# Batch 1 of an attention and feed-forward kernel: the number of h matmuls behind each of nine bursts, from a time budget to a written list

## The chip, the core and the metric

The kernel runs on one core of a Trainium2 chip. The metric is the device time of one execution in microseconds (us); the kernel before has a median of 365.38 us over three runs (364.64, 365.38, 365.54). The engines are named as in the profile: PE is the matrix engine (PEld its loading of weights), DVE the vector engine, ACT the scalar engine, POOL the GpSimd engine, SP the queue that issues stores and DMA transposes.

## The reference, cut to what matters

```python
# q, k, v: 8 batches x 12 heads x 448 rows x 64
scores = scale * q @ k.T - log(448)
attn = 1 / (1 + exp(-scores))              # a sigmoid, no softmax
attn_out = attn @ v
x = attn_out as (3584, 768)                # heads side by side
h = x @ w_in                               # w_in: 768 x 2048
g = h * (1 / (1 + exp(-h)))                # SiLU
out = g @ w_out                            # w_out: 2048 x 768
```

## The kernel before, in words

Everything is computed transposed and in 16-bit floats, with 32-bit sums in PSUM. A *group* g is four heads of one batch: three groups to a batch, 24 in all. Of a group there are seven *units* of 64 keys. A unit's `scores` (L253) are four matmuls of 64x448 into one double PSUM bank `psc`, followed by one ACT sigmoid (L267) that writes the tile `attnT`. When all seven units of a group are there, `values` (L275) multiplies them with v in 28 matmuls into two single banks `pav`; two DVE instructions (L302) then bring these into `xT`, the input of the feed-forward part.

The h matmuls of batch b come in 16 *chunks* of 128 hidden columns. `h_unit(b, fc)` (L319) is a generator: it takes one bank `ph`, issues six matmuls of 128x448 with one `yield` after each, and ahead of the last `yield` records what empties the bank. For batch 0 that is an ACT sigmoid (L337) and a DVE product (L338); for batch 1 one ACT SiLU (L342). `first_h` (L588) runs through the 16 chunks of batch 0, then the 16 of batch 1, and between chunks also records pieces of other DVE work (sums of weights, L361 and L512, and copies for later transposes, L216). A chunk of batch 1 can't finish without `xT` of groups 3, 4 and 5; `pairs` (L317) takes group 5's columns last, in the fifth and sixth matmul.

Every engine takes its instructions in the order in which the Python code records them (L53 turns the scheduler off). So the order of the calls is the order of the work. The part that the change touches is L765 to L799. At that point units 0 to 23 have their scores, and chunks 0 and 1 of batch 0 have four of six matmuls each (`begin`, L732). Then come nine *bursts*, n = 24, 26, ..., 40, each the scores of units n and n + 1. `burst` (L777) also issues `values` of a group one burst after the group's last unit: `values(3)` in burst 28, `values(4)` in burst 36; `values(5)` follows the loop at L797. Behind bursts 26 and 30 PE also transposes k and q of group 5 (14 small matmuls and two DVE copies each). Behind each burst `stretch` (L767) runs the stream of h matmuls: each is taken for 189 ns, and it goes on until the sum reaches 1600 ns per burst (900 ns ahead of the first). After `values(5)` the rest of the stream runs without a break (L798), and then the next stage begins: `sets(0)` (L607), whose first instruction on PE is the first product of `out_set` (L536, L539), with bursts of scores between its products.

PSUM has eight banks. In this stage `banks_for_attention(2)` gives two double buffers to `psc` (banks 0 to 3) and four single ones (banks 4 to 7) to all else: `ph`, `pav` and the transposes' `ptr`. A new single tile gets, of the four, the buffer whose last reader was recorded longest ago, and its first matmul waits for that reader. In the next stage `banks_for_attention(3)` (L806) leaves two single buffers, banks 6 and 7; the first product takes bank 6 and the second takes bank 7, and each waits for whoever read that bank last in the stage before.

Of the kernel before, what the change touches and what calls it, by code (L numbers as in the profile page):

```python
# [17 lines left out]
def kernel(  # L18
# [19 lines left out]
    NT_B = NQ * NCH  # L38
# [549 lines left out]
    def first_h():  # L588
        for b in range(2):
            for fc in range(NFC):  # L590
                yield from early[fc] if b == 0 and fc < 2 else h_unit(b, fc)
                if b == 0 and fc >= 10 or b == 1 and fc < 6:
                    next(in_sums)
                if b == 0:
                    continue
                if fc >= 2:
                    next(sums)
                if fc in by_h1:
                    for name in ("k", "q"):
                        dma_transpose(by_h1[fc], name, nc.vector.tensor_copy)  # L600
                    if by_h1[fc] == 8:

                        nc.gpsimd.tensor_copy(gate, qkT["q", 8][:1, 0, :1])
                        for to in (9, 10, 11):
                            load("kq", to)

    def sets(m):  # L607
        for g in range(0, NCH - 1, 2):
            step = out_set(
                block(m, g), row_blocks(m, g), block(m, g + 1), row_blocks(m, g + 1)  # L610
            )
            for i, ns in enumerate(step):
                if m == 0 and g == 0 and i in (10, 14):
                    next(sums)
                if m == 0 and g == 0 and i in (20, 28, 36, 44):
                    next(in_sums)
                yield ns
        if m % 2 == 1:
            g = NCH - 1
            yield from out_set(  # L620
                kept, row_blocks(m - 1, g), block(m, g), row_blocks(m, g), m == B // 2 - 1
            )
# [82 lines left out]
    def values_if_any():  # L705
        if waiting:
            g = waiting.pop(0)
            values(g)
            after_values(g)
            return True  # L710
        return False
# [10 lines left out]
    def transposes(g, name):  # L722
        pe_transpose(g, ((name, 0, 4), (name, 4, NCH)))
        if name == "q":
            after_transpose(g)
# [36 lines left out]
        for do, *what in behind.get(n, ()):  # L762
            do(*what)

    done = due = 0.0  # L765

    def stretch(stream, ns, spent=0):  # L767
        nonlocal done, due
        due += ns
        done += spent  # L770
        while done < due:
            step_ns = next(stream, None)
            if step_ns is None:
                return
            done += step_ns

    def burst(n, size=2):  # L777

        new = units[n : n + size]
        for u in new:  # L780
            scores(*u)
        with_values = values_if_any()
        for g, ch in new:
            if ch == NCH - 1:
                waiting.append(g)
                if 9 <= g + 3 < NQB:
                    later.extend(((g + 3, "k"), (g + 3, "q")))
        return with_values

    stream = first_h()  # L790
    stretch(stream, 900)
    for n in range(NT_B + 3, 2 * NT_B, 2):
        burst(n)
        if n in (26, 30):
            transposes(5, "k" if n == 26 else "q")
        stretch(stream, 1600)
    values_if_any()  # L797
    for _ in stream:  # L798
        pass  # L799
# [5 lines left out]
    for m in range(B // 2 - 1):  # L805
        banks_for_attention(3)  # L806
        nc.scalar.activation(warm, bias_s, AF.Sigmoid)
        stream = sets(m)
# [5 lines left out]
        n = 2 * NT_B * (m + 1)  # L814
# [59 lines left out]
```

## Time and profile before

| what | us |
|---|---|
| three runs: lowest, median, highest | 364.64, 365.38, 365.54 |
| the profiled execution, its time | 364.96 |
| its span (first to last instruction) | 363.2 |
| PE busy in the span | 355.8 (98%) |
| DVE, ACT busy | 252.8 (70%), 249.5 (69%) |
| the nine bursts: first scores of burst 24 to the first matmul of `values(5)` | 28.97 to 53.01 |
| h matmuls without a break behind `values(5)` | 54.46 to 73.96 |
| start of the next stage's first product | 73.96 |
| TensorE clock granted, all slices | 1.00 |

A row of the time-ordered view reads: start, duration, engine, line, operation, written tile <- read tiles, shapes, how many are merged; in brackets the idle time ahead of it and what ended it. A merged row's duration runs from the first start to the last end, so that rows of pipelined matmuls overlap: the next row starts before the one above it ends. The distance of two starts is therefore the better measure on PE.

### The profile page before, as it was taken

What the parts mean: (1) busy time and instruction counts of PE and PEld (TensorE: products, weight loads), DVE (VectorE), ACT (ScalarE), POOL (GpSimd) and SP (SyncE); (2) the same over time, 40 slices, a digit from 0 to 9 for tenths busy, and PEclk for the clock granted to TensorE, in tenths of its full rate; (3) what the DMA queues carried; (4) which work ended last, traced back from release to release, by engine and by line L of the source; (5) the groups of instructions that cost most, each with busy time, mean ns of one, the idle gap of its engine ahead of it and who ended that gap; (6) DMA issues with size and microseconds to landing.
All of it is one profiled execution on the core that took longest, in us unless ns stands there. A gap on an engine that the chain in (4) does not pass through costs nothing. (4 is left out here: it accounts for less than half of the span.)

```text
span 363.2 us, 7671 instructions
## 1 busy us (share of the span) xinstructions
PE 355.8 (98%) x3044; PEld 186.5 (51%) x3044; DVE 252.8 (70%) x461; ACT 249.5 (69%) x341; POOL 76.7 (21%) x115
## 2 busy tenths in 40 slices
PE   7999999999999999999999999999999999999995
PEld 5554445555555555555555455554555555556662
DVE  3665469867666587868566768795856677797763
ACT  6999886489989756688777756679899956640000
POOL 8666421040060272000032047000100000000000
PEclk9999999999999999999999999999999999999999
DMA  9999999989979599008879469602983120003333
GB/s 164 201 202 204 204 204 204 172 116 159 175 109 215 118 133 172 1 2 163 105 133 204 92 138 164 115 2 53 163 102 88 25 65 0 3 0 83 92 88 87
DMA packets 65859, 42.87 MB, mean 118 GB/s; under 512 B 35872, under 2 KB 62496, under 8 KB 65824
## 3 DMA queue, kind: packets, MB, share of 16 engines
q0 software_dynamic: 26800, 22.52, 42.0%
q1 hardware_dynamic: 38320, 19.34, 26.9%
q10 hardware_dynamic: 704, 0.52, 0.4%
q8 instruction: 24, 0.39, 0.4%
q14 instruction: 11, 0.09, 0.1%
HBM read 45.61 MB, written 11.01 MB: 156 GB/s over the span
## 5 line engine op out<-in xcount | busy, mean ns | idle before, releaser
L267 ACT ACTIVATE attnT<-psc,bias_s 128x896 f16<-128x896 f32 x166 | 156.0, 1008 | 20.1 <-PE psc L260 18.8
L539 PEld LDWEIGHTS <-S 128*128 128x128 f16 x448 | 42.0, 98 | 33.6 <-issue 8.1
L260 PE MATMUL psc<-qT,kT 64*64 64x448 f16 x664 | 48.3, 360 | 1.3 <-ACT attnT L245 0.7
L302 DVE TENSOR_SCALAR xT<-pav 128x448 f16<-128x448 f32 x48 | 27.7, 619 | 29.1 <-PE pav L291 29.1
L124 POOL DMA_DIRECT2D vf<-in_v_dram x24 | 17.3, 722 | 131.4 <-PE pav L291 110.0
L539 PEld LDWEIGHTS <-gTr 128*128 128x128 f16 x336 | 31.0, 98 | 27.3 <-issue 8.7
L539 PE MATMUL po<-w_out_sb,gTr 128*128 128x384 f16 x224 | 41.6, 327 | 0.0
L413 PEld LDWEIGHTS <-w_in_sb 128*128 128x128 f16 x288 | 27.9, 98 | 26.7 <-issue 1.1
L539 PE MATMUL po<-T,S 128*128 128x384 f16 x224 | 41.0, 327 | 0.0
L539 PE MATMUL po<-w_out_sb,S 128*128 128x384 f16 x224 | 40.8, 326 | 0.0
L323 PE MATMUL ph<-xT,w_in_sb 128*128 128x448 f16 x192 | 38.5, 353 | 0.0
L291 PE MATMUL pav<-attnT,vf 64*64 64x448 f16 x672 | 38.1, 351 | 0.1
L413 PE MATMUL pa<-xT,w_in_sb 128*128 128x448 f16 x144 | 33.1, 353 | 0.0
L260 PEld LDWEIGHTS <-kT 64*64 64x64 f16 x664 | 17.8, 104 | 27.9 <-issue 21.4
L413 PEld LDWEIGHTS <-SI 128*128 128x128 f16 x216 | 21.1, 98 | 20.0 <-issue 0.5
L291 PEld LDWEIGHTS <-vf 64*64 64x64 f16 x672 | 21.6, 106 | 12.3 <-issue 2.9
L323 PEld LDWEIGHTS <-w_in_sb 128*128 128x128 f16 x192 | 17.8, 98 | 18.9 <-issue 3.4
L429 ACT ACTIVATE part<-pa 128x448 f32<-128x448 f32 x24 | 12.8, 541 | 18.0 <-PE pa L413 18.0
L539 PE MATMUL po<-T,gTr 128*128 128x384 f16 x112 | 21.9, 327 | 0.6 <-DVE osb L560 0.6
L407 ACT ACTIVATE gTr<-pc 128x448 f16<-128x448 f32 x24 | 13.0, 543 | 12.9 <-DVE pc L423 12.5
L423 DVE TENSOR_TENSOR part<-pb,part 128x448 f32<-128x448 f32 x24 | 14.9, 621 | 8.3 <-ACT part L429 5.0
L191 ACT ACTIVATE m<-po 128x384 f32<-128x384 f32 x1 | 0.5, 490 | 27.3 <-PE po L539 27.3
(80 smaller groups left out, 473.2 us busy)
## 6 DMA issues: line engine op xcount, KB each, us to landing
out_dram<-osb SPq DMA_DIRECT2D x52, 192.0 KB, 3.2
vf<-in_v_dram POOLq DMA_DIRECT2D x24, 224.0 KB, 6.5
kf<-in_k_dram POOLq DMA_DIRECT2D x23, 224.0 KB, 6.4
qf<-in_q_dram POOLq DMA_DIRECT2D x23, 224.0 KB, 7.6
w_in_sb<-in_moe_w_in_dram POOLq DMA_DIRECT2D x16, 192.0 KB, 7.9
w_out_sb<-in_moe_w_out_dram POOLq DMA_DIRECT2D x4, 768.0 KB, 14.9
out_dram<-osb SPq DMA_DIRECT2D x6, 96.0 KB, 2.2
kT<-kr SPq DMA_TRANSPOSE x18, 4.8
```

What stands on the lines that cost most here:

```text
L124: nc.gpsimd.dma_start(flat[name, g][:, :, c0:c1].rearrange("p i c d -> p i (c d)"), rows_in(name, g)[:, :, c0 * D : c1 * D],)
L191: nc.scalar.activation(o, i, AF.Copy)
L260: nc.tensor.matmul(psc[own, j, :S], qkT["k", g][rows, ch, own], qkT["q", g][rows, :, own], start=True, stop=True,)
L267: nc.scalar.activation(attnT[g, ch], psc[:, :, :S], AF.Sigmoid, bias=bias_s, scale=QKSCALE)
L291: nc.tensor.matmul(pav[half][j * D : (j + 1) * D, :S], flat["v", g][own, j, ch, :], at[own, j, :], start=(ch == 0), stop=(ch == NCH - 1),)
L302: nc.vector.tensor_scalar_mul(xT[b][:, half * NQ + iq, :], pav[half][:, :S], SX)
L323: nc.tensor.matmul(ph[:, :S], w_in_sb[:, cc, fc * P : (fc + 1) * P], xT[b][:, cc, :], start=(at == 0), stop=(at == NCC - 1),)
L407: nc.scalar.activation(gTr[:, r * NG + i, col + c * S : col + (c + 1) * S], h, AF.Silu, bias=0.0, scale=ISX)
L413: nc.tensor.matmul(to, w[:, n, i * P : (i + 1) * P], x[:, n], start=(start and n == 0), skip_group_check=not start, stop=(n == NQ - 1),)
L423: nc.vector.tensor_add(o, po, x)
L429: nc.scalar.activation(got[i, 1], bank[i, "a"], AF.Copy)
L539: nc.tensor.matmul(po[:, :NO2], a[:, fc, :], w[:, fc, :], start=(fc == 0), stop=(fc == NHC - 1))
```

## The change

The time budget is taken out, and the counts of h matmuls are written into the loop:

```diff
-    done = due = 0.0
-
-    def stretch(stream, ns, spent=0):
-        nonlocal done, due
-        due += ns
-        done += spent
-        while done < due:
-            step_ns = next(stream, None)
-            if step_ns is None:
-                return
-            done += step_ns
-
     stream = first_h()
-    stretch(stream, 900)
-    for n in range(NT_B + 3, 2 * NT_B, 2):
+    for _ in range(5):
+        next(stream)
+    for n, count in zip(range(NT_B + 3, 2 * NT_B, 2), (9, 8, 8, 8, 10, 10, 9, 8, 9)):
         burst(n)
         if n in (26, 30):
             transposes(5, "k" if n == 26 else "q")
-        stretch(stream, 1600)
+        for _ in range(count):
+            next(stream)
     values_if_any()
     for _ in stream:
         pass
```

Nothing else differs. The counts that the budget gave follow from its arithmetic (189 ns a step against 900 + 1600 per burst):

| burst n | ahead | 24 | 26 | 28 | 30 | 32 | 34 | 36 | 38 | 40 |
|---|---|---|---|---|---|---|---|---|---|---|
| what PE does in it besides scores | | | transposes k | values(3) | transposes q | | | values(4) | | |
| h matmuls behind it, before | 5 | 9 | 8 | 9 | 8 | 9 | 8 | 9 | 8 | 8 |
| running sum, before | 5 | 14 | 22 | 31 | 39 | 48 | 56 | 65 | 73 | 81 |
| h matmuls behind it, after | 5 | 9 | 8 | 8 | 8 | 10 | 10 | 9 | 8 | 9 |
| running sum, after | 5 | 14 | 22 | 30 | 38 | 48 | 58 | 67 | 75 | 84 |

The whole stream has 184 steps (192 matmuls less the eight of `begin`); what is not issued in the loop is issued behind `values(5)`. In this count chunk fc of batch 0, from 2 to 15, ends at step 6 fc - 2: chunk 10 at 58, chunk 12 at 70, chunk 13 at 76, chunk 14 at 82, chunk 15 at 88.

## The prediction

> **What bounds the kernel now.** I read the engines' busy times first, then PE's own waits, then the bursts of batch 1 in order of time on PE, ACT and DVE, and last the seam to the next stage.
>
> ```profile
> PE 355.8 (98%) x3044; PEld 186.5 (51%) x3044; DVE 252.8 (70%) x461; ACT 249.5 (69%) x341; POOL 76.7 (21%) x115
> ```
>
> PE is busy 98% of the span, so only what makes PE wait, or spares it a wait, moves the time. These are all its waits for other engines:
>
> ```profile
> PE pw L188 <- DVE bias_s L661: 1.1, 1, 1.1
> PE psc L260 <- ACT attnT L245: 0.7, 1, 0.7
> PE po L539 <- DVE osb L560: 0.6, 1, 0.6
> PE psc L260 <- DVE qT L208: 0.3, 1, 0.3
> PE psc L260 <- ACT attnT L267: 0.2, 1, 0.2
> ```
>
> Only the last lies in the changed stretch. It is in burst 36 (PE in order of time; a gap between rows is left out):
>
> ```profile
> 43.00 1.69 PE L323 MATMUL ph<-xT,w_in_sb 128*128 128x448 f16 x8
> 44.62 0.38 PE L260 MATMUL psc<-qT,kT 64*64 64x448 f16 x4
> 45.24 0.38 PE L260 MATMUL psc<-qT,kT 64*64 64x448 f16 x4 [0.24 <-ACT attnT L267]
> 45.43 1.52 PE L291 MATMUL pav<-attnT,vf 64*64 64x448 f16 x28
> ...
> 50.81 0.65 PE L260 MATMUL psc<-qT,kT 64*64 64x448 f16 x8
> 51.39 1.69 PE L323 MATMUL ph<-xT,w_in_sb 128*128 128x448 f16 x8
> 53.01 1.52 PE L291 MATMUL pav<-attnT,vf 64*64 64x448 f16 x28
> 54.46 7.74 PE L323 MATMUL ph<-xT,w_in_sb 128*128 128x448 f16 x40
> ```
>
> The second unit's scores should start some 0.21 us behind the first's (28 matmuls of values, seven times four, take 54.46 - 53.01 = 1.45, so four take 0.207). They start 0.62 later: PE loses 0.41, of which 0.24 shows as idle. The 40 h matmuls behind values(5) give the price of one: (7.74 - 0.35) / 39 = 0.189 us, without a stall. ACT, and then DVE, over the same stretch:
>
> ```profile
> 42.42 0.98 ACT L337 ACTIVATE tx<-ph 128x448 f16<-128x448 f32 x2
> 43.26 1.93 ACT L267 ACTIVATE attnT<-psc,bias_s 128x896 f16<-128x896 f32 x2
> ...
> 49.12 1.90 ACT L267 ACTIVATE attnT<-psc,bias_s 128x896 f16<-128x896 f32 x2
> 50.92 0.54 ACT L337 ACTIVATE tx<-ph 128x448 f16<-128x448 f32 x1
> 51.34 1.92 ACT L267 ACTIVATE attnT<-psc,bias_s 128x896 f16<-128x896 f32 x2
> 53.12 0.57 ACT L337 ACTIVATE tx<-ph 128x448 f16<-128x448 f32 x1
> ```
> ```profile
> 51.49 0.62 DVE L338 SCALAR_TENSOR_TENSOR gTr<-ph,tx 128x448 f16<-128x448 f32 x1 [1.22 <-ACT tx L337]
> ...
> 53.72 0.62 DVE L338 SCALAR_TENSOR_TENSOR gTr<-ph,tx 128x448 f16<-128x448 f32 x1 [1.14 <-ACT tx L337]
> ```
>
> Burst 36 waits for burst 34's second sigmoid, which ends at 43.26 + 1.93 = 45.19; PE goes on at 45.24, a hop of 0.05. The two L338 rows empty the banks of chunks 12 (until 52.11) and 13 (until 54.34). Chunk 13 is late because its L337 sigmoid stands on ACT behind both sigmoids of burst 40. The seam:
>
> ```profile
> 73.96 2.44 PE L539 MATMUL po<-w_out_sb,gTr 128*128 128x384 f16 x14
> ```
> ```profile
> 74.16 0.54 ACT L342 ACTIVATE gTr<-ph 128x448 f16<-128x448 f32 x1 [0.59 <-PE ph L323]
> ```
>
> The next stage's first product starts 0.74 us before ACT has emptied the bank of batch 1's last chunk (74.70). That works because this chunk lies in bank 7, and the first product takes bank 6.
>
> **The change, part by part.** No instruction is added or removed: 192 h matmuls, 18 units and their evictions stay. Three h matmuls move from behind values(5) to ahead of it, one from behind burst 28 to later, and so three kinds of terms arise. Taking the Python budget out costs nothing on the chip. No DMA moves past another on SP or POOL; their order is the same, and no PE wait above is for a DMA.
>
> *1. Burst 36's stall goes: -0.41.* With one h matmul fewer behind burst 28, burst 32 starts at 40.19 - 0.19 = 40.00; with ten instead of nine behind it, burst 34 at 42.50 as now. ACT, whose chain is psc-bound at burst 32, is 0.19 earlier: burst 34's sigmoids end at 45.00 instead of 45.19. Ten instead of eight h matmuls put burst 36 at 42.50 + 2.12 + 0.38 = 45.00 and its second unit at 45.21, past 45.05. So values(4) starts at 45.40 instead of 45.43, with 58 h matmuls done instead of 56: 0.03 + 2 x 0.189 = 0.41 gained. Chunk 10 now ends ahead of burst 36, so that its L337 (0.54) stands before that burst's sigmoids on ACT, which end near 47.8; burst 38 needs them at about 48.7, so this is hidden by values(4) and nine h matmuls, and would cost at most 0.54 without them. Bounds of the term: 0 and -0.41.
>
> *2. values(5) runs into chunk 13's bank: +1.15.* Burst 40 starts at 50.81 - 0.03 = 50.78, its ACT work likewise 0.03 earlier; nine h matmuls behind it bring values(5) to 53.01 - 0.03 + 0.19 = 53.17. Ahead of it stand 84 steps instead of 81, so chunk 14 is finished and chunk 15 has already taken its bank. Before, values(5)'s two banks are those of chunks 11 and 12, free at 52.11 at the latest. Now chunk 15 has chunk 11's, and values(5) gets those of chunks 12 and 13. Chunk 13's matmuls come earlier only as PE goes: its sixth stands behind burst 40 both times, and its sigmoid behind burst 40's on ACT. So its L338 ends at 54.34 - 0.03 = 54.31, and the first matmul into the second `pav` bank can start at 54.36. The first pair into the other bank goes at 53.17, and then PE stands: 54.36 - 53.17 = 1.19 at most, 1.09 if half a step of four (0.10) was already done. I take 1.15, nearer to the upper, since the last half step runs alone at the end. Queued behind the wait are 26 of 28 values matmuls, chunk 15 and all of batch 1; nothing else feeds PE. What comes next is in time: chunk 0 of batch 1 needs chunk 14's bank (DVE done near 55.3) at 56.5, and xT of group 5 (56.9) at 57.3 and 57.5. Bounds: 0 and 1.19.
>
> *3. The first product of the next stage runs into the last chunk's bank: +0.79.* Four banks go round over the 16 chunks of batch 1, and the round now starts one step on: chunk 0 takes chunk 14's bank, 7, then 4 and 5 (values) and 6 (chunk 15). The last of 16 therefore lies in bank 6, where before it was bank 7. The program as built says the same: its first product now waits for the SiLU of batch 1's last chunk, before for that of three chunks earlier. By the rows above that SiLU ends 74.70 - 73.96 = 0.74 behind the product's start; with the hop of 0.05 PE stands 0.79. The second product (bank 7), eight steps of 0.163 later, no longer waits for it. Bounds: 0 and 0.79.
>
> Sum: -0.41 + 1.15 + 0.79 = +1.53. On the profiled execution's own 364.96 that gives 366.49 (a span of 363.2 + 1.53 = 364.7); this execution lies 0.42 under the median of 365.38, so the median to expect is 366.91. Nothing behind the seam can take it back: PE's waits after 74 us come to 0.6 in all, and a later PE makes ACT and DVE later with it.
>
> **Rivals.**
> *One of the two new waits is hidden.* For it: each rests on one order of banks, and term 2 on an ACT chain. With term 2 alone +0.74 (366.1), with term 3 alone +0.38 (365.8). Against it: term 3 has a margin of 0.79 and term 2 of over 1.0.
> *The bursts get their cover and no bank is late: not slower.* The place is values(5)'s second bank and the first product's; the mechanism is that both evictions end before PE comes. It decides from the point where chunk 13's L338 ends before 53.2, 1.1 earlier than by the rows, and the last SiLU 0.79 earlier or in another bank. Then only term 1 is left: 365.38 - 0.41 = 364.97. The 0.24 of visible idle speaks for it; ACT's order speaks against it.
> *Burst 36 stalls anyway.* Its second unit clears burst 34's sigmoid by only 45.21 - 45.05 = 0.16. Without term 1: +1.94, 367.3.
> *PE runs slower after standing.* The opening 30 filler matmuls of 128 columns (L188) take 3.38 us, where 30 x 128/448 x 0.189 = 1.62 would do: a slow start costs 1.76. If a stall of some 1 us brought that back once: 1.53 + 1.76 = +3.29, 368.7. Against it: after the 0.68 us that PE stands until 7.79, the next filler pairs of 512 columns take 0.60 and 0.60, as later ones do (0.61, 0.60), and the granted clock reads 1.00 in every slice.
> The Trainium skill, page "TensorE: Matmul & The Clock Gate", section "A second HAM failure mode: psum-queue depth-cycling", says that short idle times between groups of matmuls, from waits on PSUM banks, can make the clock gate swing, which would be this rival; the trace's one such gap does not bear it out.
>
> **How the numbers follow.** From no change a measurement of this kernel tells about 0.3%, or 1.1 us: slower means above 366.48. Forecast 0.66, one wait hidden 0.17, no wait 0.07, burst 36 stalls 0.06, slower PE 0.04. The forecast's own range is 366.4 to 367.4 (terms 2 and 3 short by 0.1 or so, medians that spread by 0.4); of its 0.66, 0.06 falls under 366.48. Slower: 0.60 + 0.06 + 0.04 = 0.70. Within: 0.06 + 0.17 + 0.05 = 0.28. Faster by over 1.1: 0.02, out of the no-wait case, since the stretch holds no more than the 0.41 and some 0.1 to gain. The range 365.8 to 367.5 takes in the forecast, the hidden wait and the stalled burst, and leaves out some 0.17.
>
> **What would show it.** Term 1: burst 36 near 45.0 in one row of eight, without idle. Term 2: values(5) broken after two matmuls near 53.2, then idle put down to DVE L338 and going on near 54.36. Term 3: the first L539 row near 75.5, 0.79 later than the h matmuls allow, its idle put down to ACT L342 (less than 0.79 shows, as pipelined ends cover 0.2). Wrong would be: values(5) in one piece, the first product 0.19 behind the last h matmul, or a span under 364.

## The result, and the profile after

| | before | after |
|---|---|---|
| median of 5 runs, us | 365.35 (364.64 to 365.54) | 366.85 (366.66 to 367.40) |
| ratio of the times, 95% interval | | 1.0045 (1.0033 to 1.0056) |
| the profiled execution, its time and span | 364.96, 363.2 | 367.40, 365.4 |
| burst 24's first scores to the next stage's first product | 28.97 to 73.96: 44.99 | 29.59 to 76.14: 46.55 |

The change makes the kernel 1.50 us slower. The last row is the fairest measure of it: inside one execution, the stretch that the change touches takes 46.55 - 44.99 = 1.56 us longer. Behind it the two traces run alike (the next bursts start 2.37 behind the first product before, 2.36 after). The other 0.6 us between the two spans lies ahead of burst 24 (29.59 against 28.97), in code that is the same; the last section comes back to it. Below, *the stretch* always means this distance.

PE's waits after: burst 36's is gone from the list, and two stand there that it didn't have.

```profile
PE pw L188 <- DVE bias_s L661: 1.1, 1, 1.1
PE pav L291 <- DVE gTr L338: 0.8, 1, 0.8
PE psc L260 <- ACT attnT L245: 0.7, 1, 0.7
PE po L539 <- ACT gTr L342: 0.6, 1, 0.6
```

PE in order of time, from burst 34 to values(4), then burst 40 and values(5), then the seam:

```profile
43.12 0.57 PE L260 MATMUL psc<-qT,kT 64*64 64x448 f16 x8
43.62 2.07 PE L323 MATMUL ph<-xT,w_in_sb 128*128 128x448 f16 x10
45.62 0.57 PE L260 MATMUL psc<-qT,kT 64*64 64x448 f16 x8
46.02 1.49 PE L291 MATMUL pav<-attnT,vf 64*64 64x448 f16 x28
...
51.38 0.65 PE L260 MATMUL psc<-qT,kT 64*64 64x448 f16 x8
51.96 1.88 PE L323 MATMUL ph<-xT,w_in_sb 128*128 128x448 f16 x9
53.77 0.38 PE L291 MATMUL pav<-attnT,vf 64*64 64x448 f16 x2
54.97 1.51 PE L291 MATMUL pav<-attnT,vf 64*64 64x448 f16 x26 [0.82 <-DVE gTr L338]
```
```profile
73.83 1.68 PE L323 MATMUL ph<-xT,w_in_sb 128*128 128x448 f16 x8
76.14 1.14 PE L539 MATMUL po<-w_out_sb,gTr 128*128 128x384 f16 x6 [0.63 <-ACT gTr L342]
```

Burst 36 is one row of eight without idle. values(5) breaks after two matmuls: the pair for the first bank goes at 53.77, the second bank's at 54.97, 1.20 later. At the seam the eight h matmuls from 73.83 would let the next instruction start at 73.83 + 8 x 0.189 = 75.34; the product starts at 76.14, 0.80 later. The bracketed idle is smaller both times (0.82 and 0.63), because the ends of pipelined matmuls cover the rest.

What ended the two waits, on DVE and on ACT:

```profile
54.30 0.62 DVE L338 SCALAR_TENSOR_TENSOR gTr<-ph,tx 128x448 f16<-128x448 f32 x1 [1.14 <-ACT tx L337]
```
```profile
51.91 1.92 ACT L267 ACTIVATE attnT<-psc,bias_s 128x896 f16<-128x896 f32 x2
53.69 1.01 ACT L337 ACTIVATE tx<-ph 128x448 f16<-128x448 f32 x2
...
75.54 0.54 ACT L342 ACTIVATE gTr<-ph 128x448 f16<-128x448 f32 x1 [0.59 <-PE ph L323]
```

The L338 row empties chunk 13's bank and ends at 54.92; PE goes on at 54.97. Its L337 sigmoid is the first of the two at 53.69, right behind burst 40's sigmoids. The last SiLU ends at 76.08; the product follows at 76.14.

### The profile page after: what moved, and what is told of

Same layout as the page of the kernel before. It is cut to its first block, busy times and chain, and to the rows that moved or that the text cites. A ratio compares the mean times of both kernels' runs of the same rounds, so it can differ in the third digit from the quotient of the medians.

```text
span 365.4 us, 7671 instructions
## 1 busy us (share of the span) xinstructions
PE 356.8 (98%) x3044; PEld 187.0 (51%) x3044; DVE 252.9 (69%) x461; ACT 249.5 (68%) x341; POOL 76.7 (21%) x115
## 5 line engine op out<-in xcount | busy, mean ns | idle before, releaser
L260 PE MATMUL psc<-qT,kT 64*64 64x448 f16 x664 | 48.1, 360 | 1.0 <-ACT attnT L245 0.7
L260 PEld LDWEIGHTS <-kT 64*64 64x64 f16 x664 | 17.7, 104 | 27.4 <-issue 20.9
L423 DVE TENSOR_TENSOR part<-pc,part 128x448 f32<-128x448 f32 x24 | 15.0, 624 | 6.1 <-PE pc L413 5.5
```

What stands on the lines that cost most here:

```text
L260: nc.tensor.matmul(psc[own, j, :S], qkT["k", g][rows, ch, own], qkT["q", g][rows, :, own], start=True, stop=True,)
L423: nc.vector.tensor_add(o, po, x)
```

## The experiments

Each run was timed beside the kernel before on the same chip (its medians there: 365.32 for runs 1 to 4, 365.03 for runs 5 to 7, 365.12 for runs 8 to 10). The stretch is the finer measure: a median differs from what its stretch says by up to 0.44 us, runs 3, 4 and 6 aside (run 5 lies 0.81 over the kernel before, its stretch 0.37), and the openings alone differ by up to 0.97 (last section). The counts named are those behind the nine bursts; the changed kernel has 9, 8, 8, 8, 10, 10, 9, 8, 9.

| run | stretch expected, us | stretch measured | median, us | ratio to before, 95% |
|---|---|---|---|---|
| before | | 44.99 | 365.35 | |
| after | | 46.55 | 366.85 | 1.0045 (1.0033 to 1.0056) |
| 1: after, 81 steps | 44.70 | 44.67 | 365.00 | 0.9993 (0.9984 to 1.0002) |
| 2: before, 84 steps | 46.54 | 46.59 | 366.89 | 1.0041 (1.0028 to 1.0055) |
| 3: after, other bank at the seam, first filler | 45.81 | 45.80 | 376.87 | 1.0317 (1.0303 to 1.0331) |
| 4: before, other bank at the seam, first filler | 45.83 | 45.83 | 376.01 | 1.0290 (1.0276 to 1.0304) |
| 5: after, chunk 13 early | 45.34 | 45.36 | 365.84 | 1.0015 (1.0005 to 1.0024) |
| 6: as 5 and 3 together, first filler | 44.60 | 44.61 | 375.31 | 1.0285 (1.0271 to 1.0298) |
| 7: chunk 13 early, 81 steps | 44.50 | 44.53 | 364.82 | 0.9991 (0.9983 to 1.0000) |
| 8: as 3, second filler | 45.81 | 45.80 | 365.74 | 1.0013 (0.9998 to 1.0027) |
| 9: as 4, second filler | 45.83 | 45.83 | 366.15 | 1.0023 (1.0009 to 1.0037) |
| 10: as 6, second filler | 44.60 | 44.61 | 364.88 | 0.9987 (0.9973 to 1.0001) |

**Run 1: take back only the three steps.**

```diff
-    for n, count in zip(range(NT_B + 3, 2 * NT_B, 2), (9, 8, 8, 8, 10, 10, 9, 8, 9)):
+    for n, count in zip(range(NT_B + 3, 2 * NT_B, 2), (9, 8, 8, 8, 10, 10, 9, 8, 6)):
```

> The changed counts up to burst 38, but 6 instead of 9 behind burst 40, so that 81 steps stand ahead of values(5) as before. I measure the stretch from burst 24's first scores to the next stage's first product, which the opening doesn't touch: 44.99 us before, 46.55 after. Theory (three separate terms): chunk 15 has not begun, so values(5) gets the banks of chunks 11 and 12 and the last chunk of batch 1 lies away from bank 6; both new waits are gone and term 1 alone is left, less about 0.12 because chunk 15 now comes 0.12 ahead of chunk 13's bank: 44.99 - 0.41 + 0.12 = 44.70, the time 0.3 under before (365.1). Rival (ten matmuls behind two bursts cost time by themselves, or gain nothing): 44.99 or more.

Both waits are gone. The stretch is 44.67, so the longer cover of bursts 32 and 34 is worth 0.32 by itself:

```profile
53.25 1.52 PE L291 MATMUL pav<-attnT,vf 64*64 64x448 f16 x28
54.70 19.77 PE L323 MATMUL ph<-xT,w_in_sb 128*128 128x448 f16 x103
74.31 2.44 PE L539 MATMUL po<-w_out_sb,gTr 128*128 128x384 f16 x14
```

values(5) is in one piece. The 103 h matmuls take 74.31 - 54.70 = 19.61 where before they took 73.96 - 54.46 = 19.50: the 0.11 is what chunk 15 loses on chunk 13's bank. So what costs time in the changed kernel is not that the bursts' counts are uneven, but what comes with 84 steps instead of 81 ahead of values(5): other banks. (Run 10 has 84 steps too and loses nothing in the stretch.)

**Run 2: put only the three steps into the kernel before** (its counts are 9, 8, 9, 8, 9, 8, 9, 8, 8; here 11 come last).

```diff
-    for n, count in zip(range(NT_B + 3, 2 * NT_B, 2), (9, 8, 8, 8, 10, 10, 9, 8, 9)):
+    for n, count in zip(range(NT_B + 3, 2 * NT_B, 2), (9, 8, 9, 8, 9, 8, 9, 8, 11)):
```

> The counts of before, but 11 instead of 8 behind burst 40, so that 84 steps stand ahead of values(5) while burst 36 still stalls. Theory (values(5)'s second bank is free at a time that ACT and DVE set, whenever PE comes): PE comes at 53.58 instead of 53.17, the bank is free at 54.39, PE waits 0.76 instead of 1.15, the product waits 0.79: 44.99 + 1.55 = 46.54, as in the changed kernel; the 0.41 of term 1 is then not worth anything in it. Rival (the prediction's own arithmetic for a stalled burst 36, where the terms add up): 44.99 + 1.94 = 46.93.

```profile
45.24 0.38 PE L260 MATMUL psc<-qT,kT 64*64 64x448 f16 x4 [0.24 <-ACT attnT L267]
...
53.58 0.38 PE L291 MATMUL pav<-attnT,vf 64*64 64x448 f16 x2
54.40 1.51 PE L291 MATMUL pav<-attnT,vf 64*64 64x448 f16 x26 [0.45 <-DVE gTr L338]
```

Burst 36 stalls as before, PE comes to values(5) 0.43 later (24.61 behind burst 24, in the changed kernel 24.18), and goes on at 54.40. In the changed kernel that point lies 54.97 - 29.59 = 25.38 behind burst 24, here 54.40 - 28.97 = 25.43. Both times it lies 3.59 behind burst 40's first scores (51.38 there, 50.81 here), and these start at nearly the same time, 21.79 and 21.84 behind burst 24. From there on ACT's three sigmoids and DVE's product set it, and not whether 9 or 11 h matmuls stand behind the burst. So nearly all of what the change gains in burst 36 is spent waiting 1.20 instead of 0.82 two bursts later: beside run 2's counts it is worth 46.59 - 46.55 = 0.04.

**Runs 3, 4 and 6: another bank for batch 1's last chunk.** A filler matmul ahead of that chunk takes the bank that would have been the chunk's (run 3 with the changed counts, run 4 with those of before, run 6 with those of run 5):

```diff
             for fc in range(NFC):
+                if b == 1 and fc == NFC - 1:
+                    keep_busy(1, P)
                 yield from early[fc] if b == 0 and fc < 2 else h_unit(b, fc)
```

> The changed kernel with one filler matmul of 128 columns (0.05) into a single bank of its own ahead of batch 1's last chunk, which so moves from bank 6 to bank 7. Theory (the first product waits for its bank): the 0.79 at the seam goes, the wait of values(5) stays: 46.55 - 0.79 + 0.05 = 45.81, time about 366.1. Rival (the product is late for another reason, such as the last SiLU's data or ACT's load of a table): 46.60.

> The kernel before with the same filler matmul at the same place, which moves batch 1's last chunk from bank 7 to bank 6. Theory: the seam's wait comes alone: 44.99 + 0.79 + 0.05 = 45.83, time about 366.2, with PE's idle ahead of the first product put down to ACT L342. Rival (the wait comes from the new counts, not from the bank): 45.04.

> The run before this with the filler matmul ahead of batch 1's last chunk: 84 steps ahead of values(5), and neither wait by theory: 45.34 - 0.79 + 0.05 = 44.60, time about 365.0. Rival (three more h matmuls ahead of values(5) cost time by themselves): above 45.2.

The stretches came out as expected, yet the kernels were 10 us slower: a miss in the making of the experiment. `keep_busy` multiplies `dummy`, and `dummy` lies in the buffer that the weight sum `T3` takes later (tag "T3", L182 and L503). With a reader so late, DVE stood before its first write there, and all its sums and copies for the next stage with it (DVE and PE in run 3):

```profile
73.99 0.56 DVE L512 TENSOR_TENSOR T<-w_out_sb 128x768 f16<-128x768 f16 x1 [14.01 <-PE pw L188]
```
```profile
80.50 0.96 PE L260 MATMUL psc<-qT,kT 64*64 64x448 f16 x8 [3.14 <-DMA qT<-qr]
81.40 0.82 PE L539 MATMUL po<-w_out_sb,gTr 128*128 128x384 f16 x2
87.05 2.08 PE L539 MATMUL po<-T,S 128*128 128x384 f16 x6 [4.83 <-DVE m L550]
```

The times of these three runs say nothing about the seam.

**Runs 8, 9 and 10: the same with operands that nobody overwrites soon.**

```diff
+                if b == 1 and fc == NFC - 1:
+                    pw = one_bank("pw")
+                    nc.tensor.matmul(pw[:, :P], w_in_sb[:, 0, :P], xT[1][:, 0, :P], start=True, stop=True)
```

> The changed kernel with one filler matmul ahead of batch 1's last chunk, this time on operands that nobody is waiting to overwrite (a piece of w_in and of xT). Theory: the stretch from burst 24 to the next stage's first product is 46.55 - 0.79 + 0.05 = 45.81, and no DVE work waits for the filler, so the time is 366.85 - 0.74 = 366.1. Rival (the 10 us of the run with the first filler came from the other bank order, not from its operand): about 376 again.

> The kernel before with that filler: batch 1's last chunk moves to bank 6, and the seam's wait comes alone. Theory: stretch 45.83, time 365.3 + 0.84 = 366.1, idle ahead of the first product put down to ACT L342. Rivals: no wait, 365.3; or about 376 again.

> The changed kernel with 9, 8 instead of 8, 9 behind bursts 38 and 40 and with that filler: 84 steps stand ahead of values(5) and both new waits are gone. Theory: stretch 44.60, time 365.3 - 0.4 = 364.9, 1.9 under the changed kernel. Rival (three more h matmuls ahead of values(5) cost time by themselves): 365.5 or more.

The 10 us are gone, so they came from the operand. With the changed counts the seam's wait disappears (run 8: stretch 45.80, 0.75 less for a filler of 0.05); with the counts of before the same filler brings it in (run 9):

```profile
72.58 1.30 PE L323 MATMUL ph<-xT,w_in_sb 128*128 128x448 f16 x6
74.50 1.79 PE L539 MATMUL po<-w_out_sb,gTr 128*128 128x384 f16 x10 [0.63 <-ACT gTr L342]
```

The six h matmuls would let the product start at 72.58 + 6 x 0.189 = 73.71; it starts at 74.50, 0.79 later. The wait goes with the bank and not with the counts. Beside the kernel before on their chip (365.12), run 8 lies 0.62 over it, run 9 1.03 over, and run 10, with neither wait, 0.24 under. Run 10's trace loses 0.17 again behind the seam: DVE waits 3.62 and 1.53 us for transposes there and is late with its sums, and the third product starts 0.51 behind the last part of the second, where the kernel before needs 0.34.

**Run 5: the same 84 steps, chunk 13 finished a burst earlier.**

```diff
-    for n, count in zip(range(NT_B + 3, 2 * NT_B, 2), (9, 8, 8, 8, 10, 10, 9, 8, 9)):
+    for n, count in zip(range(NT_B + 3, 2 * NT_B, 2), (9, 8, 8, 8, 10, 10, 9, 9, 8)):
```

> The changed counts with one h matmul moved from behind burst 40 to behind burst 38 (9, 8 instead of 8, 9). Chunk 13 ends ahead of burst 40, so its sigmoid stands on ACT before that burst's two; still 84 steps ahead of values(5), the same banks. Theory (the wait is for chunk 13's bank, and it is late for its place on ACT): the bank is free near 53.15 as PE comes near 53.1, so the 1.15 shrinks to 0 to 0.05, burst 40 loses its stretch of 0.08, the seam's 0.79 stays: the stretch is 44.99 - 0.49 + 0.05 + 0.79 = 45.34, time about 365.7. Rival (values(5) waits for its own input, the sigmoids of burst 40): these end some 0.4 later here, so the wait would grow, to 46.9.

DVE, ACT and PE in run 5:

```profile
53.02 0.62 DVE L338 SCALAR_TENSOR_TENSOR gTr<-ph,tx 128x448 f16<-128x448 f32 x1
```
```profile
51.44 0.98 ACT L337 ACTIVATE tx<-ph 128x448 f16<-128x448 f32 x2
52.29 1.93 ACT L267 ACTIVATE attnT<-psc,bias_s 128x896 f16<-128x896 f32 x2
```
```profile
53.64 1.56 PE L291 MATMUL pav<-attnT,vf 64*64 64x448 f16 x28
```

Chunk 13's sigmoid is now the second of the two at 51.44, ahead of burst 40's sigmoids. Its bank is free at 53.64, as PE arrives, and values(5) goes through in one piece, though it has the same two banks as in the changed kernel and burst 40's own sigmoids end later than there (54.22 - 51.52 = 2.70 behind the burst's start, against 53.83 - 51.38 = 2.45). So the wait is for the bank, and the place of one sigmoid in ACT's order decides it. One h matmul moved across burst 40 takes 1.19 us out of the stretch; what is left over the kernel before is the seam less the gain in the bursts.

**Run 7: everything that the runs say.**

```diff
-    for n, count in zip(range(NT_B + 3, 2 * NT_B, 2), (9, 8, 8, 8, 10, 10, 9, 8, 9)):
+    for n, count in zip(range(NT_B + 3, 2 * NT_B, 2), (9, 8, 8, 8, 10, 10, 9, 9, 5)):
```

> Counts 9, 8, 8, 8, 10, 10, 9, 9, 5: no stall in burst 36, chunk 13 early, 81 steps ahead of values(5), no filler. Theory: term 1 and burst 40's 0.08 are gained, nothing is lost: 44.99 - 0.49 = 44.50, time about 364.9, the fastest of all. Rival (values(5) now comes so early that it waits for the sigmoids of burst 40, which end near 53.7 against 53.76 where it needs them): 44.50 plus up to 0.3.

No wait is left in the stretch, and it is the shortest, 44.53. By the ratios it is 0.54% faster than the changed kernel (1.0045 against 0.9991). Its median is 0.21 under that of the kernel before on the same chip; the interval reaches 1.0000, so against the kernel before this is at the edge of what can be told.

## Why the prediction was right

*The sum.* Forecast +1.53; measured 1.56 in the stretch and 1.50 between the medians. Term by term, all counted from burst 24's first scores:

| term | forecast | measured, and from where |
|---|---|---|
| 1, burst 36 | -0.41 | -0.41: values(4) starts 16.43 behind burst 24 with 58 h matmuls done, before 16.46 with 56 (0.03 + 2 x 0.189) |
| 2, values(5)'s second bank | +1.15 | +1.18: the h matmuls behind values(5) start at 26.83 with 84 done, before at 25.49 with 81, so 26.83 - 25.49 - 3 x 0.189 = 0.77, and 0.41 of term 1 on top |
| 3, the seam | +0.79 | +0.80: 76.14 against 75.34; 0.79 in run 9 |

*Term 1's mechanism* held, and run 1 shows its worth where nothing follows it. *Term 2* was sized between a half step and a full one; the full one (1.19) was nearer. *Term 3* was exact because the row that ends the wait, the last SiLU, was already in the trace of before and doesn't depend on the change.

*What the sum hides.* Terms 1 and 2 are not independent. The second wait ends 3.59 behind burst 40's first scores, so what counts is how much PE has left to do behind that burst. Run 2 leaves out term 1, with 73 steps instead of 75 ahead of burst 40 and 11 instead of 9 behind it; its second wait is 0.82 instead of 1.20, and its stretch is longer by 46.59 - 44.99 = 1.60. The forecast's -0.41 is right as an entry in the sum, but run 2 does without it and is only 0.04 slower. The rival "burst 36 stalls anyway", priced at +1.94, is another case: the changed counts with that stall, which by this reading would make burst 40 late as well. No run has it, so its price is not shown; in the changed kernel's trace burst 36 doesn't stall.

*The other rivals.* One hidden wait and no wait: both waits showed in the trace and each answered to its own experiment. Slower matmuls after standing: behind the 0.82 us of idle the 26 matmuls of values take 1.51, as run 2's do behind 0.45, and the h matmuls up to the seam keep their distance, (73.83 - 56.42) / 92 = 0.189. The granted clock of 1.00, which the prediction also held against this rival, is a weak sign: it reads 1.00 over the slow 3.38 us of the opening too. The section that the prediction quoted from the Trainium skill ("TensorE: Matmul & The Clock Gate", section "A second HAM failure mode: psum-queue depth-cycling") speaks of idle times that come at each iteration; two single waits of this size did not slow PE, and no run here shows what many would do.

*The median.* The forecast took the profiled execution's distance to the median, 0.42, as it was. Behind the seam nothing was taken back, as it said: from the first product to the end of the span the two traces need 363.2 - 73.96 = 289.24 and 365.4 - 76.14 = 289.26. That the median of 366.85 came within 0.06 of the forecast is in part luck, for single runs of one kernel spread by 0.90 and 0.74.

## What to carry to other kernels

When buffers are handed out in recorded order, a count in one loop also decides which later instruction meets which buffer: after any move, list for each first write what emptied that buffer last and when, across the seam to the next pool too. A filler or a spacer is not free because it is short; look at who waits to overwrite its operands. And where a wait ends a fixed time behind an earlier burst, on another engine's work, coming to it sooner gains nothing: first move the late engine's work (here one sigmoid ahead of two), then give PE its cover.

## What the runs showed that I had not expected

The opening is not the same from run to run. Three rows of PE, before and then after, with code that is the same:

```profile
5.28 0.51 PE L188 MATMUL pw<-dummy 128*128 128x128 f16 x6
5.72 0.36 PE L201 MATMUL ptrq<-ident,qf 128*64 128x128 f16 x6
6.01 0.41 PE L237 MATMUL psc<-qT,kT 64*64 64x256 f16 x8
```
```profile
5.51 0.82 PE L188 MATMUL pw<-dummy 128*128 128x128 f16 x6
6.26 0.43 PE L201 MATMUL ptrq<-ident,qf 128*64 128x128 f16 x6
6.62 0.41 PE L237 MATMUL psc<-qT,kT 64*64 64x256 f16 x8
```

The same six filler matmuls take 0.51 in one execution and 0.82 in the other; by these rows the slow start, priced at 1.76 in the prediction, lasts longer in the second, and the lead of 0.6 us stays to the end. What sets its length is not shown. The first full scores (L260) start between 7.49 and 8.46 in the twelve traces, a spread of 0.97 where the runs of the kernel before spread by 0.90 in the result above. The granted clock reads 1.00 in both openings, so that row doesn't show it.

Long waits do bring slow matmuls, and here the granted clock shows it. Read in windows of 0.05 us it is 0.50 for some 10.2 us in runs 3, 4 and 6 (80.40 to 90.62, 80.22 to 90.46 and 80.87 to 91.11) and 1.00 on either side. In that time six matmuls of 384 columns take 2.08 (1.14 in the kernel before). They stand behind 4.83, 5.24 and 5.55 us of idle, but in runs 3 and 4 the clock had fallen before that idle began, in run 6 0.55 us into it. In run 3 PE stands for 3.14 us, the clock falls at 80.40, and the eight scores from 80.50 take 0.96 instead of 0.57. In run 6 (3.13 us, scores from 79.31) and run 4 (2.34 us, scores from 79.66) the clock falls only as the scores end or later, and they take 0.57.

The Trainium skill, "TensorE: Matmul & The Clock Gate", section "What's actually happening", has the clock halved after an idle window of about 3.4 us that runs freely. The half clock agrees. The length is not borne out: in run 4 PE had stood for 2.34 us only, and was at work again for 0.56 us, when the clock fell. What the window counts as idle is open. In the changed kernel, whose waits are 0.8 to 1.2 us, the granted clock reads 1.00 through the whole stretch.
